# A fused attention, routed feed-forward and gate kernel: four tiles stored plainly at the end, a gate product on GpSimd, and side steps at other units

## The chip, the cores and the metric

One NeuronCore of a Trainium2 chip runs the whole kernel. The metric is device time in microseconds (us) of one execution; the time given for a kernel is the median of several runs. The engines of the core are TensorE (PE in the rows, with PEld for its weight loads), VectorE (DVE), ScalarE (ACT), GpSimd (POOL) and SyncE (SP). Each of them takes its instructions strictly in the order in which they were issued to it. SP and POOL also issue the DMA transfers; a transfer that SP issues waits for its sources, and what SP has to issue behind it waits too.

## The reference

For x of 2048 tokens by 1024:

```
xn  = layernorm(x)
s   = attention(xn, 32 heads of 32, no mask) @ wo
r   = xn @ w_r;  idx = the 8 tokens with the largest r
y   = (silu(xn[idx] @ w_gate) * (xn[idx] @ w_up)) @ w_down      # F = 3584
b   = xn, with y * sigmoid(r[idx]) added at the rows idx
out = x + s * silu(b)
```

## The kernel before

**Attention.** Heads go in 8 groups of 4 (`g`), queries in 4 blocks of 512 (`qb`), keys in 16 tiles of 128 (`kt`). One (g, qb, kt) is a *unit*; there are 512, and (g, qb) with its 16 units is a *block* below. In each unit TensorE makes the scores of the next unit in two halves (`scores`, tile `sc`), ScalarE takes their exponential into a `pt` tile of 128x2048 (L412, two instructions of 128x1024), VectorE adds the tile to the running sum of the softmax denominator (`add`, L419) and TensorE multiplies it with the values (`values`, tile `oa`, L426). Between them TensorE gets pieces of other work: projections of later groups (`proj`, `vp`), the feed-forward of the routed tokens, and, in the last two blocks, the output projection (`wop`).

**Five `pt` buffers.** One holds the running sum of the block. When the block has ended, `fold` (unit 1 of the next block) has SP store that sum to DRAM (`a_d<-pt`, 1 MB), where GpSimd's accumulating DMAs halve it three times. The buffer comes free when the store has landed, and the fifth exponential after the first of the new block takes it. So these follow one another: the last `add` of a block, the store of its sum, and that exponential.

**The order is written out by hand.** `on(g, qb, kt, ...)` and `at(unit, ...)` put a side step at a unit, `then(n, ...)` at the n-th piece of the tail; a step that returns (k, f) has f run k units later. The order in which steps are called is the order on every engine, SP's and POOL's queues included. Within a unit the scores, the add and the values come first, then the side steps in the order of their registration.

**Router.** `route_rows`, `route_halves` and `route_best` find the eight tokens; `route_slots` (DVE L629 to L645, with a store `slot_d` on SP) makes the gate and the slot of each token, `routed_tokens` gathers the rows (POOL L650), `routed_norm` normalises them on VectorE (L658 to L662), `routed_turn` transposes them on TensorE. Before, these stood at units 2, 7, 10, 14 and 15 of block (2, 1) and 4 and 9 of block (2, 2).

**Folding a sum back.** `fold_load` (L469, on SP) reads the folded sum, `fold_rows` (L473) adds its 16 rows, `normalise` (L507) and `split_o` scale and split the block's output. For the block before (7, 0) (`b == 27`) they stand at units 9, 12, 19 and 20 of (7, 0).

**Gates.** `gate_load` loads a tile of 128 rows of x (`z`) and gathers the routed rows that belong to it; `gate_sum` normalises z on ScalarE (L820), then in steps adds the routed rows (VectorE, L823), takes a tanh (ScalarE, L827) and multiplies (VectorE, L828): z becomes 2 silu(b). The first `gate_load` stood at unit 5 of block (7, 1), its `gate_sum` at unit 10; the output projection of the first query block begins at unit 12 of it, from where a unit takes twice as long.

**The tail.** The output projection of the last two query blocks (tokens 1024 to 2047, tiles 8 to 15 of 128) is done as seven products instead of eight (`tail_items`, by sums of halves of wo and of the attention outputs). Product n of token tile tt is three pieces on TensorE, then VectorE combines its PSUM bank with rows kept in SBUF (`p1`, `g`, `u`, `h`), multiplies by the gate z and sends the result out. The products come in the order 1, 7, 4, 6, 5, 2, 3. Tiles 8 to 13 of `out` were filled with x early (`out_fill`, in block (0, 3)), and GpSimd's accumulating DMA (`added`, L950) adds z to them; for tiles 14 and 15, `x_load` reads x into SBUF, VectorE adds, and SP stores (L1007, L1016, L1038).

## Time and profile before

| | before |
|---|---|
| median of 3 runs | 1627.84 us (1625.43 to 1633.37) |
| the profiled execution | 1629.38 us |
| its span, first to last instruction | 1627.1 us |
| TensorE / VectorE / ScalarE / GpSimd busy | 98% / 88% / 73% / 10% of the span |
| mean granted TensorE clock | 0.995 |
| DMA | 309 MB, 190 GB/s on the mean |

The profile is one execution. In a row of the timeline stand the start and the busy time of an instruction, or of several alike in a row (x4), its engine, its line in the kernel, what it writes and reads, and in brackets how long its engine had been idle before it and what ended the idle time. A "q" behind an engine is its sequencer: for SP, the time to issue a transfer, not the transfer. In a row of stretches each engine has its busy time in us and in brackets its number of instructions; PEclk is the granted clock of TensorE, where 1.00 is 2.4 GHz and 0.50 is 1.2 GHz; then come the mean busy share of the 16 DMA engines and GB/s.

### The profile page before, as it was taken

What the parts mean: (1) busy time and instruction counts of PE and PEld (TensorE: products, weight loads), DVE (VectorE), ACT (ScalarE), POOL (GpSimd) and SP (SyncE); (2) the same over time, 40 slices, a digit from 0 to 9 for tenths busy, and PEclk for the clock granted to TensorE, in tenths of its full rate; (3) what the DMA queues carried; (4) which work ended last, traced back from release to release, by engine and by line L of the source; (5) the groups of instructions that cost most, each with busy time, mean ns of one, the idle gap of its engine ahead of it and who ended that gap; (6) DMA issues with size and microseconds to landing.
All of it is one profiled execution on the core that took longest, in us unless ns stands there. A gap on an engine that the chain in (4) does not pass through costs nothing.

```text
span 1627.1 us, 59437 instructions
## 1 busy us (share of the span) xinstructions
PE 1600.5 (98%) x26949; PEld 820.0 (50%) x26949; DVE 1432.0 (88%) x1195; ACT 1193.6 (73%) x1339; POOL 166.9 (10%) x163
## 2 busy tenths in 40 slices
PE   9999999999999999999999999999999999999996
PEld 7745444444455445555555555554544444444453
DVE  8478999999999999999999888887999999888886
ACT  6677777777777788888887777777888878665640
POOL 3400000100001000000000000000000002020221
PEclk9999999999999999999999999999999999999998
DMA  9946568656856676666658777778777877664686
GB/s 292 206 125 167 151 206 209 160 163 159 198 146 141 175 192 170 183 177 176 181 149 229 195 205 194 203 189 226 227 206 221 226 201 210 191 196 157 177 287 139
DMA packets 268686, 309.33 MB, mean 190 GB/s; under 512 B 109838, under 2 KB 200254, under 8 KB 264490
## 3 DMA queue, kind: packets, MB, share of 16 engines
q1 hardware_dynamic: 254298, 269.36, 56.1%
q0 software_dynamic: 14128, 36.09, 14.2%
q8 instruction: 213, 3.49, 0.9%
q14 instruction: 47, 0.39, 0.1%
HBM read 221.14 MB, written 126.41 MB: 214 GB/s over the span
## 4 chain that ended last, share of the span: by engine, by line
PE 88%; DVE 3%; DMA 3%; ACT 3%; SPq 1%; issue 1%; POOL 0%; ACTq 0%; DVEq 0%
PE sc L279 25%; PE oa L426 25%; PE proj L279 17%; PE wop L279 8%; PE vp L279 7%; PE ffn L692 1%; DVE pt L419 1%; ACT pt L412 1%; DMA a_d<-pt 1%; PE vp L328 1%; PE py L723 1%; DMA xt<-xh 1%; PE y L279 1%; DMA z<-in_A_x_dram 1%; DMA wraw<-in_A_wqkv_dram 0%
## 5 line engine op out<-in xcount | busy, mean ns | idle before, releaser
L412 ACT ACTIVATE pt<-sc 128x1024 f32<-128x1024 f32 x1024 | 997.3, 1025 | 331.5 <-PE sc L279 251.2
L419 DVE TENSOR_TENSOR pt<-pt 128x2048 f32<-128x2048 f32 x480 | 1095.4, 2285 | 66.4 <-ACT pt L412 46.7
L279 PE MATMUL sc<-qs,ks 128*32 128x512 f16 x8192 | 620.8, 380 | 9.7 <-ACT pt L412 7.9
L426 PE MATMUL oa<-pt,v 128*32 128x512 f32 x4096 | 533.2, 594 | 0.0
L279 PE MATMUL proj<-xt,w 128*32 128x512 f16 x5664 | 419.8, 379 | 0.0
L279 PEld LDWEIGHTS <-ks 128*32 128x32 f16 x8192 | 230.9, 97 | 181.3 <-issue 35.7
L279 PEld LDWEIGHTS <-w 128*32 128x32 f16 x5664 | 160.7, 97 | 234.5 <-issue 138.3
L463 POOL DMA_DIRECT2D a_d<-a_d x90 | 72.9, 810 | 1203.3 <-DMA a_d<-pt 847.4
L279 PEld LDWEIGHTS <-xt 128*32 128x32 f16 x4608 | 127.8, 97 | 103.4 <-issue 75.7
L426 PEld LDWEIGHTS oa<-pt,v 128*32 128x32 f32 x4096 | 129.8, 110 | 98.5 <-issue 0.5
L279 PE MATMUL vp<-w,xt 128*32 128x256 f16 x4608 | 173.1, 273 | 0.0
L279 PE MATMUL wop<-wo,ot 128*32 128x512 f16 x1920 | 110.4, 379 | 0.0
L279 PEld LDWEIGHTS <-ot 128*32 128x32 f16 x2112 | 59.7, 97 | 70.1 <-issue 23.2
L379 DVE SCALAR_TENSOR_TENSOR hl<-proj,hl 128x512 f16<-128x512 f32 x61 | 41.9, 688 | 28.6 <-ACT hl L378 28.1
L328 PE MATMUL vp<-w,xt 128*128 128x256 f16 x384 | 43.9, 273 | 1.6 <-DMA xt<-xh 1.1
L328 PEld LDWEIGHTS <-xt 128*128 128x128 f16 x384 | 37.1, 98 | 7.9 <-DMA xt<-xh 1.9
L378 ACT ACTIVATE hl<-proj 128x512 f16<-128x512 f32 x61 | 36.2, 594 | 1.9 <-PE proj L279 0.8
L692 PEld LDWEIGHTS ffn<-wf,xst 128*32 128x32 f32 x512 | 16.4, 110 | 38.6 <-issue 37.1
L692 PE MATMUL ffn<-wf,xst 128*32 128x224 f32 x512 | 35.8, 352 | 0.0
L279 PEld LDWEIGHTS <-sf 128*32 128x32 f16 x816 | 22.9, 97 | 19.2 <-issue 0.6
L263 DVE SCALAR_TENSOR_TENSOR w<-wraw,w 128x1024 f16<-128x1024 f32 x23 | 28.0, 1216 | 5.2 <-ACT w L258 5.2
L515 DVE SCALAR_TENSOR_TENSOR ohl<-o,ohl 128x512 f16<-128x512 f32 x24 | 16.5, 689 | 14.8 <-ACT ohl L513 14.8
(192 smaller groups left out, 751.7 us busy)
## 6 DMA issues: line engine op xcount, KB each, us to landing
a_d<-pt SPq DMA_DIRECT2D x30, 1024.0 KB
st<-hl SPq DMA_DIRECT2D x64, 256.0 KB
ks<-st SPq DMA_DIRECT2D x128, 128.0 KB
qs<-st SPq DMA_DIRECT2D x128, 128.0 KB
a_d<-a_d POOLq DMA_DIRECT2D x30, 512.0 KB, 8.7
wf<-in_B_w_gate_dram SPq DMA_DIRECT2D x32, 448.0 KB
wf<-in_B_w_up_dram SPq DMA_DIRECT2D x32, 448.0 KB
wd<-in_B_w_down_dram SPq DMA_DIRECT2D x32, 448.0 KB
```

The source lines that it names most:

```text
L263: nc.vector.scalar_tensor_tensor(hl[:, 1], WR[c, g], WS, hl[:, 0], op0=ALU.mult, op1=ALU.subtract)
L279: nc.tensor.matmul(out[c], w[:, c], x, **flags)
L328: nc.tensor.matmul(box["ps"][:, tt], xt[:, xi, k, t % 4 * P:(t % 4 + 1) * P], w[:, :, wi, k, :], start=(n == 0), stop=(n == 23))
L378: nc.scalar.activation(hl[:, 0], ps, AF.Copy, scale=KQ)
L379: nc.vector.scalar_tensor_tensor(hl[:, 1], ps, KQ, hl[:, 0], op0=ALU.mult, op1=ALU.subtract)
L412: nc.scalar.activation(PT[u][:, 2 * hf:2 * hf + 2], ps, AF.Exp, bias=0.0, scale=ESC)
L419: nc.vector.tensor_add(ACC[g, qb], ACC[g, qb], PT[u])
L426: nc.tensor.matmul(OA[g, qb][32 * j:32 * j + 32, :], VT[g, kt // 2][:, kt % 2, 32 * j:32 * j + 32], PT[u][:, j, :], start=(kt == 0), stop= ...
L463: nc.gpsimd.dma_start(a_d[0:n], a_d[n:2 * n], accum_op=ALU.add, max_dma_last_dim=4096)
L515: nc.vector.scalar_tensor_tensor(hl[:, 1], o32, OS, hl[:, 0], op0=ALU.mult, op1=ALU.subtract, accum_out=lo_f[:, n:n + 1])
L692: nc.tensor.matmul(box[i][32 * j:32 * j + 32, :], RT["xst"][:, k, :], wt[:, j * FQ:(j + 1) * FQ], start=(k == 0), stop=(k == KT - 1))
L723: nc.tensor.matmul(box["py"][32 * q:32 * q + 32, :], box["ht"][:FH, i, 32 * j:32 * j + 32], wt[:FH, q * 256:(q + 1) * 256], start=(n == 0) ...
```

## The change

- **Tail.** Tiles 12 and 13 are no longer filled early and accumulated; as tiles 14 and 15 they get x from `x_load` (four rows of x, in two `pt` tiles, at pieces 46 and 47 instead of 34 and 35), one VectorE addition per half, and a plain store. The scale WOD is applied where a bank is read (`plus`) or in ScalarE's copies, no longer in the multiplication by z. The multiplications of the low halves of the gates of the third query block (two of 128x1024) go from VectorE, in product 5, to GpSimd, in product 6.
- **Late lower halves.** For the last block, the VectorE halves of `split_o` and `form_split` run two pieces after their ScalarE halves.
- **Gates.** `gate_sum` gets a `lag`: with 2, the last multiplication comes two pieces after the tanh. The first gates move by a few units: load 4 instead of 5, sums at 12, 15, 18, 22 instead of 10, 14, 18, 22.
- **Router.** `route_best` at unit 11, and `route_slots`, `routed_tokens`, `routed_norm`, `routed_turn` at units 5, 6, 12 and 15 of block (2, 2).
- **Others.** `wo_load` and `wo_split` of the summed weights at units 1 and 6 instead of 0 and 4 of eight blocks; the fold of `b == 27` at units 11, 14, 20, 21; `form_split` one unit later.

```diff
@@ split_o
-        nc.vector.scalar_tensor_tensor(hl[:, 1], o32, OS, hl[:, 0], op0=ALU.mult, op1=ALU.subtract,
-                                       accum_out=lo_f[:, n:n + 1])
+        def lower():
+            nc.vector.scalar_tensor_tensor(hl[:, 1], o32, OS, hl[:, 0], op0=ALU.mult, op1=ALU.subtract,
+                                           accum_out=lo_f[:, n:n + 1])
+        if (g, qb) == (L, 3):
+            return 2, lower
+        lower()
@@ form_split
...
+        return (2, lower) if (g, qb) == (L, 3) else lower()
@@ gate_sum
-    def gate_sum(qb, tt):
+    def gate_sum(qb, tt, lag=1):
-            return lambda: nc.vector.scalar_tensor_tensor(z, up, 1.0, z, op0=ALU.add, op1=ALU.mult)
+            return lag, lambda: nc.vector.scalar_tensor_tensor(z, up, 1.0, z, op0=ALU.add, op1=ALU.mult)
@@ tail_items
+        def plus(to, bank, y, op=ALU.add):
+            v.scalar_tensor_tensor(to, bank, WOD, y, op0=ALU.mult, op1=op)
...
             elif n == 6 and tt % 2:
-                v.tensor_tensor(u, two, PR["p1", tt // 2], op=ALU.subtract)
+                plus(u, two, PR["p1", tt // 2], ALU.subtract)
+                v.tensor_add(h, u, h)
                 v.tensor_add(y, u, y)
-                v.tensor_add(h, u, h)
-                later.append(lambda: gated(y, GT[2][:, pair, low], WOD))
+                if tt == 3:
+                    for k in (1, 0):
+                        z = GT[2][:, 2 * k:2 * k + 2, low]
+                        nc.gpsimd.tensor_tensor(z, PR["g", k], z, op=ALU.mult)
             elif n == 5:
...
                 if tt % 2:
-                    later.pop(0)()
                     added(2, tt - 1)
                     added(2, tt)
             elif n == 2 and tt % 2:
-                v.tensor_add(two, PR["p1", tt // 2], two)
-                gated(two, GT[3][:, pair, low], WOD)
+                plus(two, two, PR["p1", tt // 2])
+                z, o = GT[3][:, pair, low], XO[tt // 2][:, :, low]
+                v.tensor_mul(z, two, z)
+                v.tensor_add(o, o, z)
                 if tt == 3:
...
             elif n == 3:
-                v.tensor_add(bank, PR["u"][:, tt], bank)
-                gated(bank, z_b[:, high], WOD)
-                if tt < 2:
-                    added(3, tt)
+                plus(bank, bank, PR["u"][:, tt])
+                v.tensor_mul(z_b[:, high], bank, z_b[:, high])
+                if tt == 1:
+                    o = XO[0]
+                    v.tensor_add(o[:, :, high], o[:, :, high], GT[3][:, pair, high])
+                    for t in range(2):
+                        nc.sync.dma_start(out[(12 + t) * P:(13 + t) * P, :], o[:, t])
...
-    def x_load(qb, tt, tag, bufs):
+    def x_load(k):
+        XO[k] = sb.tile([P, 2, D], F32, name="xo", tag="pt", bufs=PTB)
+        for n in range(2):
+            nc.sync.dma_start(XO[k][:, n], x[(12 + 2 * k + n) * P:(13 + 2 * k + n) * P, :])
...
-    for kt, f in ((2, route_rows), (7, route_halves), (10, route_best), (14, route_slots), (15, routed_tokens)):
+    for kt, f in ((2, route_rows), (7, route_halves), (11, route_best)):
         on(2, 1, kt, f)
-    on(2, 2, 4, routed_norm)
-    on(2, 2, 9, routed_turn)
+    for kt, f in ((5, route_slots), (6, routed_tokens), (12, routed_norm), (15, routed_turn)):
+        on(2, 2, kt, f)
-        on(*key, 0, wo_load, NG + g)
-        on(*key, 4, wo_split, NG + g)
-    for n in range(6):
+        on(*key, 1, wo_load, NG + g)
+        on(*key, 6, wo_split, NG + g)
+    for n in range(4):
         on(0, 3, 2 * n, out_fill, 8 + n)
-                at(nxt + (5, 3, 3)[qb] + 4 * tt, gate_load, qb, tt)
+                at(nxt + (4, 3, 3)[qb] + 4 * tt, gate_load, qb, tt)
-                    at(nxt + (10, 6, 6)[qb] + 4 * tt, gate_sum, qb, tt)
+                    at(nxt + ((12, 15, 18, 22)[tt] if qb == 0 else 6 + 4 * tt), gate_sum, qb, tt)
-                    then((4, 6)[tt - 2], gate_load, qb, tt)
-                then((0, 5, 11, 16)[tt], gate_sum, qb, tt)
+                    then((5, 7)[tt - 2], gate_load, qb, tt)
+                then((0, 4, 11, 13)[tt], gate_sum, qb, tt, 2)
-    for tt in range(4):
-        if tt > 1:
-            then(32 + tt, x_load, 3, tt, "wr", 2)
+    for k in range(2):
+        then(46 + k, x_load, k)
+                     ((1, fold), (11, fold_load), (14, fold_rows), (20, normalise), (21, split_o)) if b == 27 else
                      ((1, fold), (9, fold_load), (12, fold_rows), (19, normalise), (20, split_o))):
```

## Rows read from the trace of the kernel before

**Rows 1.** The page, part 1: busy us of each engine, share of the span, instructions.

```profile
PE 1600.5 (98%) x26949; PEld 820.0 (50%) x26949; DVE 1432.0 (88%) x1195; ACT 1193.6 (73%) x1339; POOL 166.9 (10%) x163
```

**Rows 2.** Stretches of the span: its start and end, its length, busy us and instructions of each engine, granted clock, DMA share, GB/s. The three stretches in which TensorE is idle for more than 1 us after the head.

```profile
400.00:600.00 200.00, 196.74 (x3425) 99.01 (x3417) 190.08 (x166) 156.98 (x176) 18.69 (x23) 0.99 0.69 172
1200.00:1400.00 200.00, 194.25 (x2948) 84.82 (x2944) 187.53 (x131) 160.31 (x179) 19.82 (x19) 0.99 0.81 217
1600.00:1628.00 28.00, 14.79 (x324) 8.73 (x315) 14.80 (x21) 0.00 (x0) 3.46 (x4) 0.81 0.71 146
```

**Rows 3.** Waits of TensorE: who waited for whom, us in total, times, longest. The two largest.

```profile
PE sc L279 <- ACT pt L412: 7.9, 9, 3.3
PE sc L279 <- DMA qs<-st: 1.7, 1, 1.7
```

**Rows 4.** Timeline of TensorE at the change from block (2, 1) to (2, 2).

```profile
533.33 1.04 PE L426 MATMUL oa<-pt,v 128*32 128x512 f32 x8
537.57 0.62 PE L279 MATMUL sc<-qs,ks 128*32 128x512 f16 x8 [2.76 <-ACT pt L412]
538.91 1.94 PE L426 MATMUL oa<-pt,v 128*32 128x512 f32 x8
540.60 1.11 PE L279 MATMUL proj<-xt,w 128*32 128x512 f16 x8
```

**Rows 5.** The same place on ScalarE (the exponential of the last unit of (2, 1), and the fifth after the first of (2, 2)), on VectorE (the first instruction of `route_slots`, and the four additions behind it, of which the first belongs to the last unit of (2, 1)) and on SP (the store of the sum).

```profile
516.36 1.94 ACT L412 ACTIVATE pt<-sc 128x1024 f32<-128x1024 f32 x2 [0.65 <-PE sc L279]
536.49 1.94 ACT L412 ACTIVATE pt<-sc 128x1024 f32<-128x1024 f32 x2 [4.75 <-DMA a_d<-pt]
...
523.64 0.15 DVE L629 CAST sel_i<-sel 128x1 int32<-128x1 f32 x1
525.22 9.28 DVE L419 TENSOR_TENSOR pt<-pt 128x2048 f32<-128x2048 f32 x4
...
527.67 0.38 SPq L461 DMA_DIRECT2D a_d<-pt  x1
```

**Rows 6.** VectorE: the first instructions of `routed_norm`, and the one after it. ScalarE: the exponential of the last unit of (2, 2), and the fifth after the first of (2, 3). SP: the store of the sum of (2, 2); GpSimd: the DMA that waits until it has landed.

```profile
537.22 1.27 DVE L658 BATCH_NORM_STATS2 stt<-xs 32x6 f32<-32x512 f32 x2
541.64 1.21 DVE L779 SCALAR_TENSOR_TENSOR wohl<-wo_raw,wohl 128x1024 f16<-128x1024 f32 x1
...
564.87 1.94 ACT L412 ACTIVATE pt<-sc 128x1024 f32<-128x1024 f32 x2 [0.60 <-PE sc L279]
581.26 1.95 ACT L412 ACTIVATE pt<-sc 128x1024 f32<-128x1024 f32 x2 [1.07 <-PE sc L279]
...
573.64 0.34 SPq L461 DMA_DIRECT2D a_d<-pt  x1
...
581.01 0.85 POOL L463 DMA_DIRECT2D a_d<-a_d  x1 [32.20 <-DMA a_d<-pt]
```

**Rows 7.** SP and GpSimd one block earlier: the store of the sum of (2, 0), and the DMA that waits for its landing.

```profile
481.32 0.32 SPq L461 DMA_DIRECT2D a_d<-pt  x1
...
486.63 0.81 POOL L463 DMA_DIRECT2D a_d<-a_d  x1 [31.38 <-DMA a_d<-pt]
```

**Rows 8.** The change from block (7, 0) to (7, 1). SP: a store of projected queries, the load of a folded sum, the spread of these queries. TensorE: the first scores of the block, the sum of the block's denominators (`dn`). VectorE: the addition that `dn` waits for.

```profile
1343.11 0.38 SPq L383 DMA_DIRECT2D st<-hl  x1
1352.31 0.39 SPq L469 DMA_DIRECT2D dr<-a_d  x1
1353.82 1.84 SPq L394 DMA_DIRECT2D qs<-st  x4
...
1361.10 0.61 PE L279 MATMUL sc<-qs,ks 128*32 128x512 f16 x8 [1.66 <-DMA qs<-st]
1367.99 1.04 PE L445 MATMUL dn<-pt,ones 128*32 128x512 f32 x8
...
1364.62 2.28 DVE L419 TENSOR_TENSOR pt<-pt 128x2048 f32<-128x2048 f32 x1
```

**Rows 9.** Block (7, 1). SP: the load of the first gate tile; ScalarE: its normalisation; TensorE at the same place.

```profile
1383.34 0.38 SPq L808 DMA_DIRECT2D z<-in_A_x_dram  x1
...
1392.13 1.24 ACT L820 ACTIVATE z<-z,rn 128x1024 f32<-128x1024 f32 x1 [2.42 <-DMA z<-in_A_x_dram]
...
1394.85 0.61 PE L279 MATMUL sc<-qs,ks 128*32 128x512 f16 x8 [3.25 <-ACT pt L412]
1396.25 1.04 PE L279 MATMUL sc<-qs,ks 128*32 128x512 f16 x8 [0.78 <-ACT pt L412]
1397.06 1.94 PE L426 MATMUL oa<-pt,v 128*32 128x512 f32 x8
```

**Rows 10.** The end. VectorE: the first instruction of the second pair of product 2, and the last one; GpSimd: the issue of its last accumulating DMA.

```profile
1604.45 1.23 DVE L998 TENSOR_TENSOR wop<-p,wop 128x1024 f32<-128x1024 f32 x1 [0.81 <-PE wop L279]
1615.53 0.43 DVE L1037 TENSOR_TENSOR xo<-xo,z 128x256 f32<-128x256 f32 x1
...
1612.55 0.85 POOL L950 DMA_DIRECT2D out_dram<-z  x1 [0.47 <-DVE z L946]
```

**Rows 11.** Stretches of 2 us: in the first, loads of tiles alone; the other is at the end.

```profile
1580.00:1582.00 2.00, 2.00 (x45) 1.03 (x37) 1.83 (x3) 0.14 (x1) 0.00 (x0) 1.00 1.11 397
1620.00:1622.00 2.00, 0.00 (x0) 0.00 (x0) 0.00 (x0) 0.00 (x0) 0.00 (x0) 0.50 0.40 135
```

**Rows 12.** GpSimd's additions or subtractions of 128x1024 at the head: ns minimum, median, maximum, and when.

```profile
L228 POOL TENSOR_TENSOR xh<-xin,xh x12: 2123/2131/2139, 28.2 to 65.8; 128x1024 f16<-128x1024 f32 x12
```

More of the change, by code (lines that the diff above doesn't have):

```diff
@@ L555, in form_split, with lower @@
         m = NG * NB + 2 * NG + 4 * form + i
-        nc.vector.scalar_tensor_tensor(hl[:, 1], f, OS, hl[:, 0], op0=ALU.mult, op1=ALU.subtract,
-                                       accum_out=lo_f[:, m:m + 1])
-        return 3, lambda: nc.sync.dma_start(s_d[form, i], hl)
+        def lower():
+            nc.vector.scalar_tensor_tensor(hl[:, 1], f, OS, hl[:, 0], op0=ALU.mult, op1=ALU.subtract,
+                                           accum_out=lo_f[:, m:m + 1])
+            return 3, lambda: nc.sync.dma_start(s_d[form, i], hl)
+        return (2, lower) if (g, qb) == (L, 3) else lower()
     def route_load(t):
@@ L937, in tail_items @@
         v = nc.vector
-        low, high, later = slice(0, 512), slice(512, D), []
+        low, high = slice(0, 512), slice(512, D)
         def row(name, tt):
@@ L975, in whole @@
                     PR["p1", tt // 2] = sb.tile([P, 2, 512], F32, name="p1", tag=f"w16_{tt // 2}")
-                nc.scalar.activation(PR["p1", tt // 2][:, tt % 2], bank, AF.Copy)
+                nc.scalar.activation(PR["p1", tt // 2][:, tt % 2], bank, AF.Copy, scale=WOD)
             elif n == 4:
@@ L979, in whole @@
                     PR["g", tt // 2] = sb.tile([P, 2, 512], F32, name="g", tag="qs", bufs=2)
-                v.tensor_add(PR["g", tt // 2][:, tt % 2], PR["h"][:, tt], bank)
+                plus(PR["g", tt // 2][:, tt % 2], bank, PR["h"][:, tt])
             elif n == 6 and tt % 2:
@@ L997, in whole @@
             elif n == 2 and tt % 2:
[L998 to L999 removed]
+                plus(two, two, PR["p1", tt // 2])
+                z, o = GT[3][:, pair, low], XO[tt // 2][:, :, low]
+                v.tensor_mul(z, two, z)
+                v.tensor_add(o, o, z)
                 if tt == 3:
[L1001 to L1005 removed]
+                    u, o = PR["u"][:, tt], XO[1][:, 1]
+                    v.tensor_mul(u, u, z_b[:, high])
                     v.tensor_add(o[:, high], o[:, high], u)
[L1007 removed]
+                    nc.sync.dma_start(out[S - P:S, low], o[:, low])
             elif n == 3:
[L1009 to L1014 removed]
+                plus(bank, bank, PR["u"][:, tt])
[5 more added lines that the diff above has]
+                        nc.sync.dma_start(out[(12 + t) * P:(13 + t) * P, :], o[:, t])
+                elif tt == 2:
+                    o = XO[1][:, 0]
                     v.tensor_add(o[:, high], o[:, high], z_b[:, high])
@@ L1024, in lines @@
                 row("h", tt - 1)
[L1025 removed]
+                nc.scalar.activation(PR["h"][:, tt - 1:tt + 1], PR["y", tt // 2], AF.Copy, scale=WOD)
         def last(h, j):
@@ L1029, in last @@
             to = slice(512 + 256 * h, 768 + 256 * h)
-            z, o = GT[3][:, 3], XO[3, 3]
+            z, o = GT[3][:, 3], XO[1][:, 1]
             if j == 0:
@@ L1035, in last @@
             if j == 2:
-                gated(bank[:, cols], z[:, to], WOD)
+                v.scalar_tensor_tensor(z[:, to], bank[:, cols], WOD, z[:, to], op0=ALU.mult, op1=ALU.mult)
                 v.tensor_add(o[:, to], o[:, to], z[:, to])
@@ L1049, in out_fill @@
         nc.sync.dma_start(out[t * P:(t + 1) * P, :], x[t * P:(t + 1) * P, :])
-    def x_load(qb, tt, tag, bufs):
-        t = 4 * qb + tt
-        XO[qb, tt] = sb.tile([P, D], F32, name="xo", tag=tag, bufs=bufs)
-        nc.sync.dma_start(XO[qb, tt], x[t * P:(t + 1) * P, :])
+    def x_load(k):
+        XO[k] = sb.tile([P, 2, D], F32, name="xo", tag="pt", bufs=PTB)
+        for n in range(2):
+            nc.sync.dma_start(XO[k][:, n], x[(12 + 2 * k + n) * P:(13 + 2 * k + n) * P, :])
     fill = {(g, qb): [] for g in range(NG) for qb in range(NB)}
@@ L1194, in _fast @@
     then(31, split_o, L, 3)
-    then(33, form_sum, L, 3)
-    then(34, form_split, L, 3, 0, 3)
+    then(32, form_sum, L, 3)
+    then(33, form_split, L, 3, 0, 3)
     then(41, form_tiles, SF, 4, False, "sf")
@@ L1224, in _fast @@
         elif qb == 3 and 4 <= g < L:
-            for k, f, a in ((16, form_load, ()), (25, form_sum, ()), (26, form_split, (0, 3))):
+            for k, f, a in ((16, form_load, ()), (25, form_sum, ()), (27, form_split, (0, 3))):
                 at((b + 1) * NT + k, f, g, qb, *a)
```

25 lines of the change are left out of this document (7 added, 18 removed).

## The prediction, made before the changed kernel was run

> **What bounds the kernel now.** I read the page's busy shares first, then stretches of the span, TensorE's waits, the timeline where it waits, and the end. TensorE is busy for 1600.5 of 1627.1 us [rows 1]: of the work that the change moves, only what TensorE waits for, or what stands after its last matmul, costs time. The stretches find 3.3 us idle at 400 to 600, 5.8 at 1200 to 1400 and 13.2 at the end [rows 2]. The waits name two causes in the middle: ScalarE's exponentials late (7.9 us) and one late transfer of queries (1.7) [rows 3]. The change touches each of these places. The sum is made against the profiled execution, 1629.38 us (its span and 2.28 around it), which lies 1.54 above the median.
>
> **Router.** TensorE stands 2.76 us for an exponential [rows 4], which waited 4.75 us for the buffer that the store of the last sum frees [rows 5]; ScalarE may thus be 4.75 - 2.76 = 2.0 late before TensorE feels it. Behind the wait the same eight value matmuls take 1.94 us instead of 1.04, and the eight of the projection 1.11 instead of 0.62 [rows 4]; with the scores on either side I count 1.7 lost at the lower level of the clock (1.2 GHz). Loss: 4.4.
>
> The chain: the unit's exponential ended at 516.36 + 1.94 = 518.3, its addition at 525.22 + 9.28/4 = 527.5; VectorE trailed by 9.2 us, and the store went out at once [rows 5]. The eight instructions of the slots, 523.64 to 525.22, stand right before that addition [rows 5]. Moved behind it, the store goes out 1.6 earlier, at about 526. It then took 8.8 us (527.67 to ScalarE's start at 536.49) [rows 5]; one block earlier 5.3 [rows 7], one later 7.4 [rows 6]. With about 8.2, it lands 2.2 earlier, and 0.5 of the 2.76 is left; at the two ends 0 and 1.1. I take 0.5, no loss of clock.
>
> But the moved work lands in block (2, 2), ahead of the same kind of store. There VectorE trailed by 573.64 - 566.81 = 6.8 us at the store [rows 6], with the normalisation (537.22 to 541.64, 4.4 us) already in it, and only because TensorE's 4.4 lost us gave VectorE as much time. Without that loss the trail is 6.8 + 4.4 = 11.2: the store leaves at 566.8 + 11.2 = 578.0 on the old clock and lands after 5.3 to 7.4 us, at 583.3 to 585.4, where ScalarE was due at 581.3 [rows 6, 7]. It is 2.0 to 4.1 late, and TensorE loses 0 to 2.1; the transposes of the routed rows, now three units behind the normalisation instead of five, may add some tenths. I take 1.0, since the later store finds less queued before it; other end 2.1 + 0.5 + 1.7 at the low level = 4.3. Router: -4.4 + 0.5 + 1.0 = **-2.9** (+1.0 to -4.4).
>
> The gather of the routed rows goes behind GpSimd's three DMAs of the fold: it has six units until the normalisation. I price it at nothing; if it is late, VectorE and the transposes stand for the rest.
>
> **Queries and the fold.** SP stood from 1343.5 to 1352.31 at the load of a folded sum, with the spread of the queries behind it (out from 1353.82), and TensorE lost 1.66 at the block's start [rows 8]. Two units later (some 5 us) that load stands behind the spread, which goes out when due; the stall goes. Next late is the sum of denominators: TensorE reached it at 1367.99, 1.66 earlier it is at 1366.33, and its last addition ends at 1364.62 + 2.28 = 1366.9 [rows 8]. **-1.1** (-0.6 to -1.7).
>
> **First gate.** z was issued at 1383.34 and landed at 1392.1; ScalarE, in order, stood 2.42 us before its exponentials, TensorE 3.25 + 0.78, and the eight value matmuls behind took 1.94 again [rows 9]: 1.3 at the low level, 5.3 in all. One unit earlier the load leaves at some 1381, lands near 1390, and ScalarE comes two units later, in a unit of double length, near 1394. The wait goes. Next late is VectorE, which adds 2.28 per unit [rows 8] and was busy 187.5 of these 200 us [rows 2], so that ScalarE may come to wait for its additions instead, at most the same 2.4: **-4.7** (-2.3 to -5.4). The tile's last multiplication comes three units behind, in front of the product that reads it in order; VectorE waits there, TensorE has a third PSUM bank to go on with.
>
> **End.** VectorE loses two instructions of 1.2 us in product 5 (to GpSimd) and two short waits for ScalarE, and gains 1.2 in product 2 and 1.2 in product 3. Before, it had caught up at the second pair of product 2 (idle 0.81 for TensorE [rows 10]); it still does, so the former are worth nothing, and the addition in product 3 (a 1024-wide one takes 1.23 [rows 10]) makes its last instruction end at 1615.96 + 1.2 = 1617.2. Stores: before, two accumulating DMAs of 512 KB leave by 1613.4 [rows 10] and the DMA engines are busy for 0.8 of 1620 to 1622 [rows 11], traffic thus ending near 1621.5 and the span 5.6 later. After, four plain 512, 512, 512 and 256 KB follow from 1613.5: 1.84 MB at the 397 GB/s of rows 11 are 4.6 us; from 1615 they end near 1619.6, 2.4 us behind VectorE's last instruction. I take **-2.0**; the other end is +1.2, if that instruction sets the end. The x rows are issued eleven pieces of 16 matmuls ahead of their first use, 176 x 14.79/324 = 8.0 us [rows 2]; four of 512 KB are 5.3 us at that rate.
>
> GpSimd's two multiplications are bounded by 2.13 each [rows 12], beside VectorE, from nothing to 4.3. I take nothing: in product 5 VectorE's instructions read a PSUM bank and one tile. The Trainium skill ("SBUF — State Buffer", "Who interferes with whom") says that a VectorE instruction with two SBUF inputs stands while GpSimd reads SBUF, one with a single SBUF input does not. By that rule the price here is nothing; had product 5 two SBUF inputs, 4.3 would use up the cover and make the end some 1.0 later. No row before shows such a pair side by side.
>
> The tail's gates, late halves and scales move no matmul: TensorE has none of its waits there [rows 3], and it runs on from bank to bank. `wo_load` one unit later: nothing, but see the last rival. Fewer early fills: nothing, TensorE did not wait there.
>
> **Sum.** -2.9 - 1.1 - 4.7 - 2.0 = -10.7: 1629.4 - 10.7 = 1618.7 on the profiled execution, 1627.8 - 10.7 = **1617.1** as a median. Own range 1613.5 to 1620.5. A difference within 0.5%, 8.1 us, is about what a measurement of this kernel can't tell from none; the border is 1619.7.
>
> **Rivals.**
> - *The router's loss moves to the next block whole.* For it: 11.2 of trail is more than the 9.2 that cost 4.4 [rows 5]. Against: the shorter transfers of rows 6 and 7. Gives back 2.9: **1620.0** (at its end 1621.0).
> - *VectorE, not the transfers, sets the end.* For it: its last instruction moves 1.2. Against: busy DMA engines to 1621 [rows 11]. Gives back 2.0 and 1.2: **1620.3**.
> - *The gate's wait is only replaced.* ScalarE stands for VectorE's additions instead, so the edit doesn't do what it says. Gives back 2.4: **1619.5**; with the clock staying low once more, 1621.
> - *Slower: the sums' stores land late at eight blocks.* The load of 512 KB of summed weights, one unit later, stands directly ahead of the store in SP's queue. In rows 6 the store landed at 581.0; ScalarE was due at 581.3, so TensorE feels it from 583.3. The slowest store here took 8.8, the fastest 5.3 [rows 5 to 7]: 3.5 more at eight places is 8 x (3.5 - 2.3) = 9.6, with low clock of 1.7 at half of them 16.4: 1617.1 + 16.4 = **1633.5**. It decides from 10.7/8 + 2.3 = 3.6 us later on, without the clock. Against: moved by one unit, (564.87 - 516.36 - 4.4)/16 = 2.8 us [rows 5, 6], the load can't well hold a store back by more than that.
>
> **Chances.** Forecast 0.42, router 0.25, end 0.13, gate 0.10, slower 0.10. The first is under the border in five of six, the two at 1620 in about a third, the gate in half: 0.53, cut to 0.50 for what I don't see; slower about two thirds of the last, and some of what was cut: 0.09; within 0.5%: 0.41. The range reaches down to all upper gains (-4.4, -1.7, -5.4, -2.5 are -14) and up to the middle cases together with a late store at some blocks: 1613 to 1626.5.
>
> **What would show it.** Router: no idle above 1 us on TensorE after the first five units of (2, 2), and at most 1 in (2, 3); wrong if 2 or more stands there under ScalarE waiting for the store. Queries: SP issues the spread within 5 us of the store. Gate: no wait of ScalarE for z, and no eight value matmuls of 1.9 us there. End: VectorE's last instruction some 2.4 us behind TensorE's last matmul (1614.8 before, rows 2), the span ending within 10 us of it. It is wrong as a whole if TensorE's busy stretch shrinks by less than 6 us.

## The result, and the profile after

The changed kernel takes 1639.04 us, median of 10 runs (1634.53 to 1647.22); the kernel before, on the same chip, 1627.86. The ratio is 1.0064, with a 95% interval of [1.0046, 1.0082]: some 10 us slower. The forecast was 1617.1 us, in a range up to 1626.5, with a chance of 0.09 for slower. The profiled execution took 1636.83 us. Of all runs here and below a single one fell in a slow state, one of e9 (2101.94 us), and it is left out of its median.

The page, part 1 [rows 1]; the stretches [rows 2]; the waits of TensorE [rows 3], all of the changed kernel:

```profile
PE 1603.3 (98%) x26949; PEld 814.9 (50%) x26949; DVE 1431.7 (88%) x1194; ACT 1194.2 (73%) x1339; POOL 164.6 (10%) x163
```

```profile
400.00:600.00 200.00, 190.67 (x3281) 93.31 (x3273) 182.24 (x160) 150.99 (x169) 17.05 (x21) 0.98 0.65 162
1200.00:1400.00 200.00, 198.10 (x3044) 87.11 (x3040) 187.56 (x130) 162.59 (x183) 17.25 (x19) 1.00 0.79 214
1400.00:1500.00 100.00, 95.58 (x1552) 45.11 (x1548) 82.19 (x62) 59.86 (x63) 13.17 (x13) 0.97 0.54 166
1600.00:1636.00 36.00, 26.28 (x536) 15.62 (x528) 26.36 (x35) 0.00 (x0) 8.48 (x6) 0.94 0.74 206
```

```profile
PE sc L279 <- ACT pt L412: 7.7, 7, 4.1
PE wop L279 <- DMA wo<-wo_d: 4.4, 2, 2.7
PE xsp L678 <- DVE xs L672: 2.7, 1, 2.7
PE wop L279 <- DMA tf<-t_d: 2.2, 1, 2.2
```

The wait for the queries is gone, and three waits are new: for `wo`, for `xs`, for `tf`. In the stretch from 400 to 600 TensorE is idle for 9.3 us instead of 3.3; from 1200 to 1400 for 1.9 instead of 5.8, but then for 4.4 from 1400 to 1500.

**The router.** Timelines of TensorE, ScalarE, SP, GpSimd and VectorE in (2, 2) and (2, 3) [rows 4 to 6]:

```profile
539.18 1.05 PE L279 MATMUL sc<-qs,ks 128*32 128x512 f16 x8 [4.11 <-ACT pt L412]
565.59 0.62 PE L279 MATMUL sc<-qs,ks 128*32 128x512 f16 x8 [1.60 <-ACT pt L412]
575.82 0.68 PE L678 MATMUL xsp<-ident,xs 32*128 32x32 f32 x8 [2.65 <-DVE xs L672]
577.03 1.08 PE L279 MATMUL sc<-qs,ks 128*32 128x512 f16 x8
...
538.10 1.94 ACT L412 ACTIVATE pt<-sc 128x1024 f32<-128x1024 f32 x2 [6.20 <-DMA a_d<-pt]
...
528.02 0.38 SPq L461 DMA_DIRECT2D a_d<-pt  x1
...
538.31 0.86 POOL L463 DMA_DIRECT2D a_d<-a_d  x1 [35.13 <-DMA a_d<-pt]
543.86 0.78 POOL L463 DMA_DIRECT2D a_d<-a_d  x1 [4.69 <-DMA a_d<-a_d]
549.00 0.77 POOL L463 DMA_DIRECT2D a_d<-a_d  x1 [4.35 <-DMA a_d<-a_d]
549.52 0.44 POOL L646 IOTA ti<- 128x16 int32 x1
...
549.99 0.17 DVE L648 CAST tf<-ti 128x16 f32<-128x16 int32 x1 [5.57 <-POOL ti L646]
```

The wait that was to shrink to 0.5 grew from 2.76 to 4.11. Then VectorE stands 5.57 us for `ti`, sixteen columns of numbers that depend on nothing: GpSimd makes them only behind the fold's three accumulating DMAs, of which the first waits for the store of the sum and each other for the landing of the one before. At 565 TensorE waits for ScalarE, which had stood 2.25 us for a load of `wo_raw` that SP issued behind the slots' store. At 575 it waits for VectorE, which is late, and low clock follows: scores take 1.08 us instead of 0.61, and the granted clock is 0.67 on the mean of 575.8 to 581.0, where 0.50 is the lower level and 1.00 the upper.

**(7, 1)** [rows 9], SP and TensorE: ScalarE no longer waits for `z`, TensorE waits for weights of the output projection:

```profile
1372.57 0.32 SPq L483 DMA_DIRECT2D r_d<-dr  x1
...
1386.56 0.32 SPq L453 DMA_DIRECT2D dr<-d_d  x1
...
1401.58 0.56 SPq L488 DMA_DIRECT2D rb<-r_d  x1
...
1404.07 1.04 SPq L810 DMA_DIRECT2D wo<-wo_d  x2
...
1408.82 0.83 PE L279 MATMUL wop<-wo,ot 128*32 128x512 f16 x12 [2.68 <-DMA wo<-wo_d]
1411.39 2.33 PE L279 MATMUL wop<-wo,ot 128*32 128x512 f16 x20 [1.74 <-DMA wo<-wo_d]
```

**The tail**, VectorE, SP and TensorE. The addition of the gate summed at piece 11 waits 3.69 us for its gathered rows, the last gate's, at piece 13, 2.25 for ScalarE; the reciprocal of the last block's sums is queued behind both; SP's loads of `tf` stand behind the spread that needs the reciprocal:

```profile
1577.82 1.23 DVE L833 TENSOR_TENSOR z<-z,up 128x1024 f32<-128x1024 f32 x1 [3.69 <-DMA up<-y_d,slot_i]
...
1581.30 1.23 DVE L833 TENSOR_TENSOR z<-z,up 128x1024 f32<-128x1024 f32 x1 [2.25 <-ACT z L830]
...
1584.17 0.25 DVE L479 RECIPROCAL dr<-dr 128x16 f32<-128x16 f32 x1
...
1588.63 3.47 SPq L902 DMA_DIRECT2D tf<-t_d  x4
...
1594.98 7.95 PE L279 MATMUL wop<-tf,sf 128*32 128x512 f16 x144 [2.21 <-DMA tf<-t_d]
```

**The end** [rows 10, 11]: VectorE's last instruction, and stretches of 2 us:

```profile
1628.16 0.42 DVE L1051 TENSOR_TENSOR xo<-xo,z 128x256 f32<-128x256 f32 x1
```

```profile
1628.00:1630.00 2.00, 0.00 (x0) 0.00 (x0) 0.56 (x2) 0.00 (x0) 0.00 (x0) 1.00 1.00 382
1630.00:1632.00 2.00, 0.00 (x0) 0.00 (x0) 0.00 (x0) 0.00 (x0) 0.00 (x0) 0.86 0.36 120
```

VectorE ends 2.3 us behind TensorE (1626.3), the transfers at 1630.7, the span at 1635.1: 8.8 behind TensorE instead of 12.3.

### The profile page after: what moved, and what is told of

Read it like the earlier page. It is cut to its first block, busy times and chain, and to the rows that moved or that the text cites. A ratio compares the mean times of both kernels' runs of the same rounds, so it can differ in the third digit from the quotient of the medians.

```text
span 1635.1 us, 59470 instructions
## 1 busy us (share of the span) xinstructions
PE 1603.3 (98%) x26949; PEld 814.9 (50%) x26949; DVE 1431.7 (88%) x1194; ACT 1194.2 (73%) x1339; POOL 164.6 (10%) x163
## 4 chain that ended last, share of the span: by engine, by line
PE 84%; DVE 6%; DMA 5%; issue 1%; SPq 1%; ACT 1%; POOL 0%; DVEq 0%; ACTq 0%; POOLq 0%
PE sc L279 24%; PE oa L426 24%; PE proj L279 17%; PE wop L279 7%; PE vp L279 7%; DVE pt L419 3%; PE ffn L702 1%; DMA a_d<-pt 1%; PE vp L328 1%; PE py L733 1%; DMA xt<-xh 1%; PE y L279 1%; DMA r_d<-dr 0%; DMA wraw<-in_A_wqkv_dram 0%; DMA wo<-wo_d 0%
```

## The experiments

In this table every length is read from one profiled execution: from the first exponential of a block to that of the next named one; the tail from the last exponential to the end of the last matmul; the end from there to the end of the span. The kernels are named by their labels; c0 is the changed kernel run once more. The last column has the median, and the ratio to the kernel before as measured beside it (its medians were 1627.2 to 1627.9).

| kernel | (2,2)+(2,3) | (3,0)-(5,0) | (7,0) | (7,1) | tail | end | median us, ratio |
|---|---|---|---|---|---|---|---|
| before | 92.2 | 353.2 | 42.6 | 49.1 | 68.3 | 12.3 | 1627.86 |
| changed | 100.6 | 351.7 | 40.8 | 52.4 | 70.7 | 8.8 | 1639.04, 1.0064 |
| c0 changed again | 99.5 | 351.7 | 40.8 | 49.7 | 73.2 | 8.7 | 1637.94, 1.0075 |
| e1 router back | 91.4 | 351.7 | 40.8 | 47.3 | 73.1 | 8.6 | 1628.38, 1.0001 |
| e2 iota early | 94.2 | 352.1 | 40.8 | 46.3 | 73.0 | 8.7 | 1633.34, 1.0029 |
| e3 fold back | 98.0 | 351.9 | 40.8 | 44.6 | 74.7 | 8.7 | 1632.73, 1.0029 |
| e4 tail gates back | 97.9 | 352.3 | 40.8 | 50.3 | 68.3 | 8.7 | 1630.67, 1.0013 |
| e5 three back | 91.2 | 351.7 | 40.8 | 44.5 | 68.3 | 8.7 | 1618.10, 0.9941 |
| e7 e5, gate back | 92.0 | 351.7 | 40.8 | 45.3 | 68.3 | 8.8 | 1619.06, 0.9945 |
| e10 e5, best later | 90.8 | 351.7 | 40.8 | 44.5 | 68.3 | 8.7 | 1618.17, 0.9940 |
| e11 e5, norm later | 92.0 | 352.2 | 40.8 | 44.5 | 68.3 | 8.6 | 1618.60, 0.9946 |
| e12 e5, slots, norm later | 96.7 | 351.7 | 40.8 | 44.8 | 68.3 | 9.1 | 1622.63, 0.9974 |
| e13 e12, iota early | 90.9 | 352.2 | 40.8 | 44.7 | 68.3 | 9.7 | 1617.80, 0.9935 |
| e16 e13, norm next block | 88.8 | 356.1 | 42.1 | 48.6 | 68.3 | 8.8 | 1619.12, 0.9948 |
| e17 e13, turn next block | 91.3 | 351.7 | 40.8 | 44.5 | 68.3 | 9.1 | 1618.13, 0.9939 |
| e6 before, end alone | 92.4 | 353.3 | 41.6 | 49.9 | 68.3 | 8.7 | 1624.70, 0.9973 |
| e8 before, form_split | 94.4 | 353.3 | 40.8 | 45.3 | 68.3 | 11.6 | 1624.65, 0.9982 |
| e9 before, wo_load | 91.4 | 351.7 | 40.8 | 46.7 | 68.3 | 11.8 | 1625.72, 0.9987 |
| e14 before, gate | 92.5 | 353.3 | 40.8 | 46.6 | 68.3 | 12.2 | 1626.74, 0.9990 |
| e15 before, fold | 92.0 | 353.3 | 40.8 | 51.4 | 68.3 | 13.4 | 1630.31, 1.0020 |

### One part undone

```diff
# e1: the router's units of before; e2, in the changed kernel:
@@ route_best
+        ti = small.tile([P, NT], I32, name="ti", tag="ti", bufs=1)
+        nc.gpsimd.iota(ti, pattern=[[P, NT]], base=0, channel_multiplier=1)
+        RT["ti"] = ti
@@ route_slots
-        nc.gpsimd.iota(ti, pattern=[[P, NT]], base=0, channel_multiplier=1)
+        ti = RT["ti"]
# e3
-                     ((1, fold), (11, fold_load), (14, fold_rows), (20, normalise), (21, split_o)) if b == 27 else
# e4
-                    then((5, 7)[tt - 2], gate_load, qb, tt)
-                then((0, 4, 11, 13)[tt], gate_sum, qb, tt, 2)
+                    then((4, 6)[tt - 2], gate_load, qb, tt)
+                then((0, 5, 11, 16)[tt], gate_sum, qb, tt)
```

> The changed kernel with the five router steps back at their old units (best 10, slots 14, tokens 15 of (2,1), norm 4 and turn 9 of (2,2)), all else as changed. Theory: the moved router steps cost 8.0 us (the first exponential of (3,0) comes 8.7 us later than before, 0.7 of it from the head), so the time falls to about 1631, and (3,0) begins within 1 us of the kernel before. Rival: the loss at blocks (2,2) and (2,3) has another source in the change (wo_load and wo_split one and two units later stand in these blocks too); then 2 us or less come back: 1637 or more.

> The changed kernel with one GpSimd instruction moved: the iota of the token numbers (ti) is issued in route_best instead of route_slots, ahead of the fold's three accumulating DMAs instead of behind them; the router's units stay as changed. Theory: the 5.6 us that VectorE stands for ti in (2,2) carry most of the router's loss, because the slot store, the load of wo_raw on SP behind it, the normalisation and the transposes of the routed rows all follow from it: the wait goes, TensorE's waits of 0.6 and 1.6 in the middle of (2,2) and of 2.7 for xs in (2,3) go too, 5 us (3 to 7) come back: about 1634. Rival A: VectorE had slack there and only the SP order and the position of the normalisation count: less than 1.5 us come back, the wait for xs stays above 2. Rival B: the 4.1 us wait of TensorE at the start of (2,2), which the iota does not touch, is where the loss comes from; then the same.

> The changed kernel with the fold of block (7,0)'s predecessor back at units 9, 12, 19 and 20 of (7,0), all else as changed. Theory: normalise one unit later held the single rb buffer, so SP stood for it at the next spread and the loads of the output projection's weights behind it came 4.4 us too late for TensorE: that wait goes, the wait for queries of 1.7 comes back: net 2.7 faster, about 1636. Rival: the weights are late because of the gate's load and sums at their new units; then the 4.4 stay, the 1.7 comes on top: about 1641.

> The changed kernel with the last block's gates back at their old pieces (loads at 4 and 6, sums at 0, 5, 11, 16, last multiplication one piece after the tanh). Theory: the later loads of z (pieces 5 and 7) and the gate sums that wait for them push the reciprocal, the spread rb and SP's loads of the form tiles behind it by 3 to 4 us, which TensorE feels as 2.2 us of waiting for tf: that wait goes and 2.2 us come back, about 1637. Rival: tf is late because x_load, at pieces 46 and 47, or the late lower halves hold SP or the buffers: the wait of 2.2 stays, and the time is within 1 us of the changed kernel.

> The changed kernel once more, unedited, beside the three others. It tells how far the places of loss vary between two executions of the same kernel: the kernel with the fold put back and the one with the tail's gates put back both also showed (2,2) and (2,3) 2.6 us shorter in all, a place that their edits don't touch. Theory: the total is 1639 again, and (2,2) with (2,3) lies between 97.5 and 101 us, so that a difference of 2 to 3 us between two profiles at one place is no sign of an edit, while 8 us is. Rival: a faster chip or a better moment in the last call; then the total falls to about 1635.

All four theories held as to place and sign, and the gains were as large as expected or larger: 10.7, 5.7, 6.3 and 8.4 us. The repeated run c0 explains part of it: its total is the same again, but `tf` was 3.0 us late instead of 2.2, and the tail 73.2 long instead of 70.7. One profile had shown the tail's loss at its smallest. The single figures don't add up: those of e1, e3 and e4 make 25.4, and the three undone together bring back 20.9 (e5, below). Nor do the traces split them cleanly: in e1 9.2 us are gone from the router's two blocks, but (7, 1) is 5.1 shorter and the tail 2.4 longer, where its edit does nothing.

The router's four units cost most. The iota alone gives back about half of that, by one instruction placed earlier. With the fold back, SP's chain in (7, 1) runs 5.4 us earlier at `dr`, 8.3 at `rb` and 9.2 at the last weights, from the same block start (1367.5 in both traces), and TensorE doesn't wait for `wo`:

```profile
1366.42 0.32 SPq L483 DMA_DIRECT2D r_d<-dr  x1
...
1381.16 0.32 SPq L453 DMA_DIRECT2D dr<-d_d  x1
...
1393.33 0.55 SPq L488 DMA_DIRECT2D rb<-r_d  x1
...
1394.91 1.06 SPq L810 DMA_DIRECT2D wo<-wo_d  x2
```

That `rb` waited for its single buffer, as my expectation had it, isn't so: at that spread the changed kernel's SP waits for the landing of `r_d` (2.8 us). The chain is late from its first link on. SP has to send `r_d`, the reciprocals of the shifted fold, and stands 5.4 us until VectorE has them. That store leaves 5.0 us behind the block's start, in all six kernels with the shifted fold; with the fold back SP stands as long (5.0), but the store leaves 1.1 ahead of the start. The wait for queries, which e3's theory had coming back, did not: (7, 0) is 40.8 long.

### Three parts back, and single parts on the kernel before

e5 puts back together what e1, e3 and e4 put back one by one, e7 the first gate too. e6, e8, e9, e14 and e15 put one part of the change into the kernel before: the end; then

```diff
# e8 form_split, three lines such as
-(25, form_sum, ()), (26, form_split, (0, 3))
+(25, form_sum, ()), (27, form_split, (0, 3))
# e9
-        on(*key, 0, wo_load, NG + g)
-        on(*key, 4, wo_split, NG + g)
+        on(*key, 1, wo_load, NG + g)
+        on(*key, 6, wo_split, NG + g)
# e14: gate_load (4, 3, 3), gate_sum (12, 15, 18, 22)[tt]; e15: the line of b == 27
```

> The changed kernel with three parts back as before: the router's units, the fold of the block before (7,0), and the tail's gates. Kept: the first gate's move, the plain stores, GpSimd's product, the late lower halves, wo_load at unit 1, form_split one unit later. Theory: the three losses are separate, each was shown by undoing it alone, and the parts that are kept gain: with the blocks' lengths as the runs with one part undone show them (48.3 and 43.1 for (2,2) and (2,3), 44.6 for (7,1), 68.3 for the tail up to TensorE's last matmul, 8.7 behind it) the median comes to 1617, between 1614 and 1621, below both kernels. Rival: the losses hide one another (a stall taken away at the router only makes the next one longer, as the tail's grew from 70.7 to 73 to 75 us where an earlier one was undone); then it ends at 1624 or more.

> The kernel before with the end alone changed: tiles 12 and 13 loaded, added and stored plainly, the scale moved to the readers of the banks, two products on GpSimd; all units as before. Theory: what stands behind TensorE's last matmul falls from 12.3 to 8.7 us, and nothing else moves: 3.6 us faster, 1624.2. Rival: the transfers of x at pieces 46 and 47 or GpSimd's products delay something ahead of the last matmul; then the end is 8.7 but the time falls by less than 1.5 us.

> As the kernel with three parts back, with the first gate back too (load at unit 5, sums at 10, 14, 18, 22 of (7,1)). Theory: ScalarE waits for z again as before, and (7,1) is longer than in the kernel with three parts back by the 4.7 that the prediction took: 49.1 against 44.6 us; the time is 1621 to 1622. Rival: without the fold's shift the load of z lands in time at either unit; then both kernels agree within 1.5 us.

e5 came to 1618.10, 0.9941 [0.9929, 0.9953], faster than both kernels. So the three parts cost 20 to 21 us together, and the others gain 9.5. The end alone gained 2.9, as expected. For the first gate the rival held: with the gate back, (7, 1) is 45.3 long, not 49.1. What shortened it then? e6 has the old gate, too; ScalarE and VectorE there:

```profile
1389.98 1.25 ACT L828 ACTIVATE z<-z,rn 128x1024 f32<-128x1024 f32 x1
1393.13 0.63 ACT L558 ACTIVATE shl<-ft 128x512 f16<-128x512 f32 x1 [1.91 <-DVE ft L548]
...
1392.41 0.68 DVE L548 TENSOR_TENSOR ft<-o,ft 128x512 f32<-128x512 f32 x1
```

Here `z` was in time, and ScalarE stood for the next instruction, `form_split`'s. In the kernel before, the same pair stands a few lines behind the wait that I had read [rows 9]:

```profile
1393.28 0.61 ACT L554 ACTIVATE shl<-ft 128x512 f16<-128x512 f32 x1
...
1391.32 0.69 DVE L544 TENSOR_TENSOR ft<-o,ft 128x512 f32<-128x512 f32 x1
```

`ft` ended at 1392.0 and `z` came at 1392.1: two waits of the same end, of which the profile names one. And `z`'s wait does not belong to the old units: in the five other kernels with the first gate at them ScalarE waits 0.59 for `z` (e15), 0.10 (e6) or not at all (e7, e8, e9). The length of (7, 1) also moves without an edit there: it is 49.9 in e6 and 46.7 in e9.

> The kernel before with form_split one unit later alone (27 for 26, 30 for 29), which the prediction took for nothing. Theory: in (7,1) ScalarE waited 2.42 us for z, but the next instruction, form_split's shl, needs VectorE's sum ft, which ended at 1392.0, as late as z: with the end alone changed z was early and ScalarE waited 1.91 for ft instead, with the same 3.3 us lost by TensorE. So this edit and not the gate's move holds most of that gain, and the gate's move alone would gain nothing. Where z lands in time, (7,1) falls from 49.1 to about 45.3, where z is late it stays: 2 to 4 us faster in the median, 1624 to 1626. Rival: z's late landing is the cause; then the same as before within 1 us.

> The kernel before with the loads of the summed weights at unit 1 and their splits at unit 6 of eight blocks alone, priced at nothing in the prediction. Theory: it takes away small idle times at several block starts: (3,0) to (5,0) lasted 353.2 us before and 351.7 in every kernel with this edit, so 1.5 us (1 to 2) faster, 1626.3. Rival: what a rival of the prediction held, the load now stands ahead of the store of the sums in SP's queue, which then lands late: 0 to 10 slower, and (3,0) to (5,0) is not shorter.

> The kernel before with the first gate's move alone (load at unit 4, sums at 12, 15, 18 and 22). Theory: ScalarE then waits at unit 10 of (7,1) for VectorE's ft (form_split), about 1.9 to 2.4 us, TensorE loses its 3 to 4 us as before, and the time is 1627 within 1 us. Rival, the prediction's step: 4.7 us faster, 1622.5.

> The kernel before with the fold of the block before (7,0) at units 11, 14, 20 and 21 alone. Theory: the spread of the queries goes out when due (1.1 to 1.7 us gained at (7,1)'s start), but r_d, rb and the spread behind it come later and the weights of the output projection with them: TensorE waits for wo in (7,1), which comes to 50 to 53 us; the time is 0 to 4 us slower, 1627 to 1631. Rival, the prediction's step: 1.1 faster, 1626, no wait for wo. Second rival: the weights are late only because the first gate's load goes ahead of them; then also 1626.

e8: 0.9982 [0.9973, 0.9991], (7, 1) 45.3: the edit that I had priced at nothing gains 2.6 us. e14: 0.9990 [0.9978, 1.0002]: the gate's move by itself can't be told from nothing, and the first row below shows the wait that took the place of `z`'s. e9: 0.9987 [0.9976, 0.9999], 1.5 us faster, and (3, 0) to (5, 0) is 1.0 to 1.6 shorter in every kernel with this edit but e16. e15: 1.0020 [1.0009, 1.0031], 2.8 us slower. The theory's sign was right and its mechanism wrong, for TensorE doesn't wait for `wo` there. VectorE's reciprocal stands 2.01 us for `dr` (0.42 before), VectorE reaches `ft` 32.1 us behind the block's start (29.5 before), ScalarE waits for `ft` after `z`, and TensorE loses 3.46 (the other rows). In the changed kernel, where `form_split` comes later, the same lateness reached the weights instead. Such lateness needs no shifted fold: in e16, below, TensorE waits 2.7 for `wo` with the fold at its old units, in a trace that is its slowest run (1624.26).

```profile
1391.69 0.63 ACT L554 ACTIVATE shl<-ft 128x512 f16<-128x512 f32 x1 [1.79 <-DVE ft L544]
```

```profile
1382.48 0.25 DVE L479 RECIPROCAL dr<-dr 128x16 f32<-128x16 f32 x1 [2.01 <-DMA dr<-d_d]
...
1392.70 0.63 ACT L554 ACTIVATE shl<-ft 128x512 f16<-128x512 f32 x1 [1.56 <-DVE ft L544]
...
1394.29 1.04 PE L279 MATMUL sc<-qs,ks 128*32 128x512 f16 x8 [3.46 <-ACT pt L412]
```

### The router's steps one by one, on top of e5

```diff
# e10: route_best at 11. e11: routed_norm 12, routed_turn 15 of (2, 2).
# e12: route_slots 5, routed_tokens 6, routed_norm 12, routed_turn 15 of (2, 2)
# e13: e12 with e2's edit. e16: e13 with
+    on(2, 3, 4, routed_norm)
+    on(2, 3, 9, routed_turn)
# e17: e13 with routed_turn at unit 4 of (2, 3)
```

> The kernel with three parts back, and of the router route_best alone moved again, to unit 11 of (2,1); slots, tokens, normalisation and transposes at the old units. Theory: the transfers of route_best on SP go out 3 us later and with them what stands behind; the wait for the buffer at the start of (2,2) grows from 2.3 to about 4, 1.5 us slower: 1619.6. Rival: none of the router's loss is here, since the slots' eight VectorE instructions ahead of the last addition are what makes the store late: within 0.7 us of the kernel with three parts back (1618.1).

> The kernel with three parts back, and of the router the normalisation and the transposes alone moved again, to units 12 and 15 of (2,2). Theory: the transposes three units behind the normalisation instead of five wait 2.7 us on TensorE for VectorE's last step, which trails by three units at that place, with some 1.7 us of low clock behind: (2,2) and (2,3) grow from 91.1 to 94 to 96 us, the time to 1621 to 1623. Rival: VectorE trails only because it stood 5.6 us for the iota; without that wait the normalisation ends before the transposes are due, and the time is within 1 us of 1618.1.

> The kernel with three parts back, with route_slots, routed_tokens, routed_norm and routed_turn at their new units (5, 6, 12, 15 of (2,2)) and route_best at its old one. Theory: the slots behind the fold's accumulating DMAs in GpSimd's queue carry the loss; VectorE stands 5 to 6 us for ti, (2,2) and (2,3) come to 97 to 100 us instead of 91.1 and the time to 1625 to 1628. Rival: it takes route_best's later transfers as well (they hold SP at the store of the sum); then less than 4 us slower than 1618.1.

> As the kernel with the slots and the normalisation later, with the iota ti issued in route_best, ahead of the fold's DMAs on GpSimd. Theory: VectorE doesn't stand for ti, TensorE waits neither in the middle of (2,2) nor for xs, and 5 to 6 us come back: 1619 to 1622, so within 3 us of the kernel with three parts back. Rival: without the iota's wait the gather, also behind the fold's DMAs, makes the normalisation late; then TensorE waits for xs all the same and less than 2 us come back.

By their medians both single moves cost nothing, 1618.17 and 1618.60 beside e5's 1618.10, so neither theory is borne out; with four runs each, a cost of 1.5 to 3 us can't be excluded. e10's trace does show a loss, in (2, 1), which the table leaves out: ScalarE stands for `sel`, which SP's moved transfers bring, and the block is 45.3 long instead of 43.5.

```profile
520.29 0.20 ACT L641 ACTIVATE gate<-sel 128x1 f32<-128x1 f32 x1 [2.32 <-DMA sel<-pk_d]
```

The slots with the normalisation cost 4.5 us, less than the theory's 7 to 10 (VectorE stands 4.59 for `ti`), and with the iota early -0.3: all of the 4.5 was the iota. TensorE still waits 1.7 for `xs` in e13 (2.8 in e12), against its theory. What the changed kernel lost beyond that needs `route_best` besides. No run adds that move alone to e13, but e2 differs from e13 only by it and by parts that stand far behind, and its (2, 2) and (2, 3) are 3.3 longer. The store of the sum at the start of (2, 2), and the exponential that waits for it, in e13 (`route_best` at 10; the block starts at 518.8):

```profile
518.94 11.62 DVE L419 TENSOR_TENSOR pt<-pt 128x2048 f32<-128x2048 f32 x5
...
525.99 0.34 SPq L461 DMA_DIRECT2D a_d<-pt  x1
...
534.89 1.94 ACT L412 ACTIVATE pt<-sc 128x1024 f32<-128x1024 f32 x2 [3.41 <-DMA a_d<-pt]
```

and in e2 (`route_best` at 11; 519.5):

```profile
519.84 11.62 DVE L419 TENSOR_TENSOR pt<-pt 128x2048 f32<-128x2048 f32 x5
...
527.50 0.59 SPq L784 DMA_DIRECT2D wo_raw<-t_f  x1
528.18 0.38 SPq L461 DMA_DIRECT2D a_d<-pt  x1
...
538.19 1.94 ACT L412 ACTIVATE pt<-sc 128x1024 f32<-128x1024 f32 x2 [6.01 <-DMA a_d<-pt]
```

The third of the five additions is the block's last; it ends at 525.9 in e13 and at 526.8 in e2. The store leaves at the later of two times: the end of that addition, and SP's turn. In e13 it leaves with the addition, in e2 1.4 later, behind a load of `wo_raw`. Moving the slots made the first time earlier, moving `route_best` made the second later. In e10 the store left 7.5 behind the block's start (8.7 in e5), since the block itself had begun later by the wait for `sel`: there the move's cost lies ahead of the block.

> As the kernel with the slots and the normalisation later and the iota early, but normalisation at unit 4 and transposes at unit 9 of (2,3), one block behind their old place. Theory: with the slots behind the store of the sum the wait at the start of (2,2) is gone, and with the normalisation behind the next store nothing is late in (2,3) either: 44.9 and about 43.5 us, 88.4 instead of 91.1, the time 1615 to 1616. Rival: the normalisation's 4.4 us on VectorE make the store of the sum late at the block after it wherever they stand: then the loss appears at the start of (3,0), and the time is 1617 to 1619.

> As the kernel with the slots and the normalisation later and the iota early, but with the transposes alone at unit 4 of (2,3). Theory: TensorE doesn't wait for xs (1.7 us and 0.8 of low clock), (2,3) falls from 46.0 to about 44, the time is 1616. Rival: the normalisation at unit 12 still makes the store of the sum late and the wait moves to ScalarE's fifth exponential of (2,3): (2,3) stays at 46 and the time at 1618.

Both rivals held. In e13, (2, 2) is 44.9 long instead of 48.6 before, and (2, 3) is 46.0 instead of 43.5. With the normalisation a block later, (2, 3) is well, and ScalarE waits 4.17 for the store in (3, 0); with the transposes alone later, it waits 3.74 for VectorE. The 4.4 us of the normalisation make a store late at both new places: it leaves 11.0 behind the start of (2, 3) in e13 (6.4 in e5), and 8.6 behind the start of (3, 0) in e16 (5.7 in e5). e5, e13 and e17 can't be told apart.

## Why the prediction was wrong

**Router: -2.9 predicted, +8.4 in the trace (+7.3 in c0), 10.7 when undone.** Two steps failed. "The gather of the routed rows goes behind GpSimd's three DMAs of the fold ... I price it at nothing": I followed the gather and left out the iota that `route_slots` issues ahead of it in the same queue, for which VectorE stands in order, with the sum's additions behind it. And "the store goes out 1.6 earlier, at about 526" counted VectorE alone, not SP's queue, into which `route_best` was moved. Where both are taken away (e13), the steps come out: the store leaves 1.6 earlier in the block (7.2 behind its start, 8.8 before), (2, 2) gains 3.7 (3.9 predicted), and the loss in the next block is 2.4 (1.0 taken, 0 to 4.3 the ends). So the first rival's mechanism, the loss that moves on, is there too: 1.3 are left of the 2.9, and beside e5, with the router's old units, e13 gains nothing that can be told from none.

**Queries: -1.1.** The stall that I read is not in most traces: (7, 0) is 40.8 long in 11 of the 13 other kernels that have the fold at its old units, and 41.6 and 42.1 in e6 and e16. There is mostly nothing to gain, and the shift costs 2.8 alone and 6.3 in the changed kernel. I had asked only what the load's new place frees, not what comes later with it: `r_d`, for which SP stands until 5.0 us into (7, 1), and with it `rb`, `dr`, and all that SP has behind them.

**First gate: -4.7.** "The wait goes" is right, but of the six traces with the gate at its old units only the one that I read has that wait at its full 2.42 us, and the move is worth 0.7 to 1.0, neither clear of noise. "ScalarE may come to wait for its additions instead" named the right engine; it was `form_split`'s sum, with 1.79 us in e14, so the rival by which the wait is only replaced is nearer to what happened. `form_split` one unit later, not priced, was the edit that gains there (2.6).

**End: -2.0.** Right as to the mechanism; measured 2.9 as a median, 3.6 in the traces. VectorE's last instruction was to end 2.4 behind TensorE's last matmul (2.3 measured), the traffic 2.4 behind that (2.1). Mis-sized was the rest, 5.6 carried over from before: the span ended 4.4 behind the last traffic. GpSimd's two products took 2.37 each, where the bound taken from another operation was 2.13 [rows 12], and cost VectorE nothing: its instructions with one operand in PSUM and one in SBUF last 0.69 beside them as elsewhere. By the rule of the Trainium skill ("SBUF — State Buffer", "Who interferes with whom") a VectorE instruction with at most one SBUF input, outside the modes that use two ports, does not contend with GpSimd. The trace agrees; no instruction with two SBUF inputs ran beside them.

```profile
1606.44 4.74 POOL L1000 TENSOR_TENSOR z<-g,z 128x1024 f32<-128x1024 f32 x2 [7.34 <-DVE wop L956]
...
1604.06 0.69 DVE L1005 SCALAR_TENSOR_TENSOR z<-wop,z 128x512 f32<-128x512 f32 x1
1607.92 0.69 DVE L1005 SCALAR_TENSOR_TENSOR z<-wop,z 128x512 f32<-128x512 f32 x1
```

**Tail: "The tail's gates ... move no matmul".** They cost 2.4 to 6.4 us in the table, 8.4 as a median when undone. I had looked for waits of TensorE before the change, found none, and put the term at nothing without asking what the moved sums stand ahead of. The last gate's sum, at piece 13 instead of 16, now stands ahead of the reciprocal (piece 16) on VectorE, and the sum before it waits for the rows of a gate that is loaded later (piece 5 instead of 4). With the gates back (e4) the order is the old one, and nothing waits there:

```profile
1575.85 0.24 DVE L479 RECIPROCAL dr<-dr 128x16 f32<-128x16 f32 x1
1576.15 1.23 DVE L833 TENSOR_TENSOR z<-z,up 128x1024 f32<-128x1024 f32 x1
```

The reciprocal starts 28.6 to 29.6 us behind the last exponential in the five kernels with the new gates, 22.6 to 25.0 in the fifteen others, and only the five wait for `tf`, 2.2 to 3.5 us. The rest of the tail's loss is low clock: the 144 matmuls behind that wait take 7.95 us in the changed kernel's trace, 9.64 in c0 and 10.60 in e3 (granted clock 1.00, 0.82 and 0.74 there).

**The slower rival** is not what made the kernel slower: the sums' stores didn't land late, since (3, 0) to (5, 0) became 1.5 shorter with `wo_load` one unit later, another gain that I had taken for nothing.

**The sum.** The three parts that lose cost 20 to 21 us together. That e5's 1618.1 lies near the forecast of 1617.1 is luck: it gains by the end, and by `form_split` and `wo_load`, which I had priced at nothing; of the other three terms it has only the first gate's move, which gains little.

What stays open: which of the tail's gate edits (loads, sums or lag) the loss needs, for e4 puts all of them back; and why the wait for `tf` varies between 2.2 and 3.5 from one trace to the next.

## What to carry to other kernels

List each instruction that a moved step issues, on every queue, and what that queue must finish first; an instruction that depends on nothing can still be the late one behind DMAs that wait for one another. Where one wait goes, look a few rows on for a second that ends at the same time, and see in a second execution whether the first is there at all. Judge an edit beside a tight store by both of its gates, the data and the turn in the queue.
